# Listing's narrow one-hot tile with the position innermost becomes one with the position outermost, on one Trainium2 core

## The chip, the cores and the metric

One core of a Trainium2 chip runs the whole program. The metric is device time in microseconds (us) of one execution. PE is the matrix engine, PEld its weight loads, DVE, ACT and POOL the vector, scalar and GpSimd engines, SP the engine that issues most DMAs.

## The reference

```python
def reference(**kwargs):                      # x: 8 x 3072 x 256
    attn_out = real(fft(fft(x, axis=1), axis=2))
    x = attn_out.reshape(24576, 256)
    x = elu(x @ w_in) @ w_out                 # d_ff = 2048
    return _moe2_ref(x, w_gate, w1, w2)

def _moe2_ref(x, w_gate, w1, w2):             # 8 experts, d_ff = 1024
    cap = N // E                              # 3072 tokens per expert
    order = np.argsort(-(x @ w_gate).flatten())
    for idx in order:                         # greedy: best pair first, while the expert has room
        tok, e = int(idx) // E, int(idx) % E
        if assigned[tok] >= 0 or counts[e] >= cap:
            continue
        assigned[tok] = e
        counts[e] += 1
    for e in range(E):
        mask = assigned == e
        out[mask] = np.maximum(x[mask] @ w1[e], 0.0) @ w2[e]
    return out
```

## The kernel before

`moe1` (to about 1,990 us of the span) computes the Fourier transforms and the first layer pair and leaves the router's numbers in the tile `L` (token p + 128 j lies in partition p, column j, of 192 columns). `moe2` then does the experts one after another. For each of the eight rounds there are two streams of small work besides the matrix work:

- `select(i)` finds the round's expert and its threshold by bisection and gives every chosen token its rank in the expert's list. Line 393 and 394 split the rank into `ri` (rank modulo 128) and `qi` (rank divided by 128, below 24), which become `rb` and `qb`.
- `listing(i)` turns the ranks into a list: entry (r, q) of the result `idx` must be the number of the token with rank 128 q + r. It does so with one-hot tiles and matrix products, in 12 chunks `c` of 16 columns j. The wide tile `oh` (128 x 16 per partition, line 479) is 1 where r equals the token's `rb`. The narrow tile `oq` is 48 x 16 per partition: entries 24 to 47 are 1 where q equals the token's `qb` (line 473), entries 0 to 23 are that times the column number j (`jb`, line 474), and last entries 24 to 47 are multiplied in place by the partition number (`pcol`, line 475). `place` (line 452) then does 16 matrix products per chunk, one for each j, with `oh[:, :, j]` as weights (128 columns) and `oq[:, :, j]` as the operand that streams (48 columns), summed in PSUM.

In listing 0 nothing else runs on PE: POOL does line 474, the tiles are taken from the pool `ex` (names hh, hl, yh, yl), and one bank sums all 12 chunks. In listings 1 to 7 DVE does line 474, `oq` and `oh` have two buffers each in the pool `rt`, and the chunk's sum is added to `pj` at line 457. The product of chunk c is issued after the one-hots of chunk c + 1.

The order of the work around listings 1 to 7 is written out by a simple clock: `expert(i)` issues the products of an expert (line 553 into the hidden layer, 594 to 596 out of it) and, after each few, takes a step of `listing` or `select` if the clock's costs (`dve(750)`, `act(450)`, ...) say that their engines are free. These costs are constants in the code, so the order on each engine is fixed when the program is built. Line 531 transposes gathered tokens (`yg`), line 571 makes the low half `hl` of the hidden layer on DVE, line 434 and 440 split weights on POOL.

Of the kernel before, what the change touches and what calls it, by code (L numbers as in the profile page):

```python
# [11 lines left out]
BF16 = mybir.dt.bfloat16  # L12
I32 = mybir.dt.int32
U16 = mybir.dt.uint16
AF = mybir.ActivationFunctionType
OP = mybir.AluOpType
# [5 lines left out]
NJ = N // 128  # L22
# [139 lines left out]
def moe2(tc, yd, R, w1, w2, out):  # L162
    nc = tc.nc
# [4 lines left out]
    with ExitStack() as ctx:  # L168
        con = ctx.enter_context(tc.tile_pool(name="con2", bufs=1))
        ctx.enter_context(nc.allow_low_precision(reason="counts up to 2048 are exact in float16"))  # L170
        rt = ctx.enter_context(tc.tile_pool(name="rt", bufs=1))
        wp = ctx.enter_context(tc.tile_pool(name="wp", bufs=1))
        ex = ctx.enter_context(tc.tile_pool(name="ex", bufs=2))
# [4 lines left out]
        def rps(shape, dtype=F32):  # L178
            return psum.tile(shape, dtype, name="rps")

        pcol = con.tile([128, 1], F32, name="pcol")
        tri = con.tile([128, 128], BF16, name="tri")
        onesb = con.tile([128, NJ], BF16, name="onesb")
        io16 = con.tile([128, 128, 16], BF16, name="io16")
        jb = con.tile([128, NJ], BF16, name="jb")
# [38 lines left out]
        def small(name, w=1, dtype=F32, bufs=2):  # L224
            return rt.tile([128, w], dtype, name=name, bufs=bufs)
# [20 lines left out]
        def act(d):  # L246
            ck.act = max(ck.act, ck.pe + 200) + d

        def dve(d, after=0):
            ck.dve = max(ck.dve, ck.pe + 200, after) + d  # L250
# [3 lines left out]
        def after():  # L254
            return max(ck.dve, ck.act) + AF0

        def select(i):
# [99 lines left out]
            for g in range(2):  # L357
                for c in range(2):
                    nc.tensor.matmul(tt[:, 2 * g + c:2 * g + c + 1], ge[:, g, 96 * c:96 * c + 96], onesb[:, 0:1],
                                     start=True, stop=True)  # L360
# [19 lines left out]
            u1, u2 = rt.tile([128, NJ], F32, name="u1"), rt.tile([128, NJ], F32, name="u2")  # L380
# [7 lines left out]
            yield after()  # L388
            while i - 1 in st and not st[i - 1]["listed"]:
                yield None  # L390
            ri = rt.tile([128, NJ], I32, name="ri")
            qi = rt.tile([128, NJ], I32, name="qi")
            nc.vector.tensor_scalar(ri, ui, 127, None, op0=OP.bitwise_and)
            nc.vector.tensor_scalar(qi, ui, 7, None, op0=OP.arith_shift_right)
# [1 line left out]
            qb = rt.tile([128, NJ], BF16, name="qb")  # L396
# [16 lines left out]
        def listing(i):  # L413
            while i not in st:
                yield None
            rb, qb, wix = (st[i][n] for n in ("rb", "qb", "wix"))
            wr = [wp.tile([128, 2 * FE], F32, name="wr%d" % a) for a in range(2)]
            for a, src in enumerate((w1.rearrange("e (p c) f -> (e p) (c f)", c=2),
                                     w2.rearrange("e (p c) d -> (e p) (c d)", c=8))):
                nc.gpsimd.indirect_dma_start(out=wr[a], out_offset=None, in_=src,  # L420
                                             in_offset=bass.IndirectOffsetOnAxis(ap=wix[:, 0:1], axis=0))
            fetched = ck.pe
            pj = small("pj", 48)
            prev = None
            while now[0] < i - 1:
                yield None
            wsp = [wp.tile([128, 2 * FE], F32R, name=n, bufs=2) for n in ("w1h", "w1l", "w2h", "w2l")]

            def split():
                for c in range(2):  # L430
                    rv = wr[0].rearrange("p (c f k) -> p c k f", c=2, k=8)[:, c]
                    hv, lv = (t.rearrange("p (c k f) -> p c k f", c=2, k=8)[:, c] for t in wsp[0:2])
                    nc.scalar.activation(hv, rv, AF.Copy)
                    (nc.gpsimd if i else nc.vector).tensor_tensor(lv, rv, hv, op=OP.subtract)
                    act(950)
                    yield after()
                for c in range(2):
                    ws = slice(1024 * c, 1024 * c + 1024)
                    nc.scalar.activation(wsp[2][:, ws], wr[1][:, ws], AF.Copy)
                    nc.gpsimd.tensor_tensor(wsp[3][:, ws], wr[1][:, ws], wsp[2][:, ws], op=OP.subtract)  # L440
                    act(950)
                    yield after()

            parts = split()

            if i == 0:
                pl0 = psum.tile([128, 48], F32, name="acc20")

            def place(c, oh, oq):
                pl = rps([128, 48]) if i else pl0  # L450
                for j in range(16):
                    nc.tensor.matmul(pl, oh[:, :, j], oq[:, :, j], start=j == 0 and (i > 0 or c == 0),  # L452
                                     stop=j == 15 and (i > 0 or c == NC - 1))
                if i == 0:
                    return
                if c:
                    nc.vector.tensor_tensor(pj, pl, pj, op=OP.add)
                else:
                    nc.vector.tensor_copy(pj, pl)

            for c in range(NC):
                js = slice(16 * c, 16 * c + 16)
                if i:
                    oh = rt.tile([128, 128, 16], BF16, name="oh", bufs=2)
                    oq = rt.tile([128, 48, 16], BF16, name="oq", bufs=2)
                else:
                    oh = ex.tile([128, 128, 16], BF16, name=("yh", "yl")[c % 2])
                    oq = ex.tile([128, 48, 16], BF16, name="h%s%d" % ("hl"[c % 2], c // 2), bufs=1)

                def row(a, n):  # L470
                    return a[:, js].unsqueeze(1).to_broadcast([128, n, 16])

                nc.vector.tensor_tensor(oq[:, 24:48], io16[:, 0:24], row(qb, 24), op=OP.is_equal)
                (nc.vector if i > 0 else nc.gpsimd).tensor_tensor(oq[:, 0:24], oq[:, 24:48], row(jb, 24), op=OP.mult)
                nc.scalar.activation(oq[:, 24:48], oq[:, 24:48], AF.Copy, scale=pcol)
                dve(750)
                act(450)
                yield 0
                nc.vector.tensor_tensor(oh, io16, row(rb, 128), op=OP.is_equal)
                if prev:  # L480
                    place(*prev)
                prev = (c, oh, oq)
                dve(1300)
                if ck.pe > fetched + WAIT:
                    next(parts, None)
                yield after()
            place(*prev)
            while ck.pe < fetched + WAIT and i and not draining[0]:
                yield None
            if i:  # L490
                yield from parts
            st[i]["listed"] = True
            while now[0] < i - 1:
                yield None
            idx = small("idx", 24, I32)
            if i == 0:
                nc.vector.tensor_copy(pj, pl0)
            nc.vector.scalar_tensor_tensor(idx, pj[:, 0:24], 128.0, pj[:, 24:48], op0=OP.mult, op1=OP.add)
            plan[i] = dict(idx=idx, wr=wr)
            plan[i]["w"] = wsp  # L500
            if i:
                ahead()
            else:
                fetch(*queue.pop(0))
                out_y[0] += 1
            dve(100)
            yield after()
            yield from parts
# [4 lines left out]
        def ahead():  # L513
            while queue and out_y[0] < 3 and queue[0][0] in plan:
                fetch(*queue.pop(0))
                out_y[0] += 1

        def fetch(i, g):
            y = ex.tile([128, 4, YW], F32, name="yg", bufs=3)
            plan[i]["y", g] = y  # L520
            for t in range(4):
                nc.gpsimd.indirect_dma_start(
                    out=y[:, t], out_offset=None, in_=yd,
                    in_offset=bass.IndirectOffsetOnAxis(ap=plan[i]["idx"][:, 4 * g + t:4 * g + t + 1], axis=0))
# [90 lines left out]
        class Stream:  # L615
# [9 lines left out]
            def step(self):  # L625
# [6 lines left out]
                return False  # L632

        sel_s = Stream(select, E)
        lst_s = Stream(listing, E)

        def ready(i):
# [656 lines left out]
```

## Time and profile before

| | |
|---|---|
| time, median of 3 runs (lowest to highest) | 3475.95 us (3472.55 to 3478.8) |
| the profiled execution | 3493.99 us, its span 3492.2 us |
| busy share of the span: PE, PEld, DVE, ACT, POOL | 96%, 89%, 76%, 65%, 18% |
| chain that ended last, by engine | PE 85%, DVE 6%, ACT 4% |
| that chain's share on line 452 (into `rps`) | 3% |
| granted clock, mean over the span | 0.977 |

Busy time is the union of an engine's instructions; matrix products overlap in the pipeline, so a product's own duration is longer than its distance from the next one. "The distance" below is from the start of one product to the start of the next. [...] A row of the timeline merges equal neighbours: "x16" are 16 instructions, and the duration beside it runs from the start of the first to the end of the last.

### The profile page before, as it was taken

How to read it: one execution, taken by the hardware profiler on the slowest of the kernel's cores; microseconds unless marked ns; L12 is line 12 of the kernel's file. 1: busy time of each engine (PE TensorE's matmuls, PEld its weight loads, DVE VectorE, ACT ScalarE, POOL GpSimd, SP SyncE). 2: the span in 40 equal slices, each digit the busy share in tenths (PEclk: the TensorE clock that was granted, in tenths of full speed). 3: DMA queues.
4: the chain of work that ended last, by engine and by line, in shares of the span. 5: the costliest groups of instructions: out<-in, count | busy, mean ns of one | idle time of the engine just before them, and what ended most of it. 6: DMA issues, size and time to landing. Idle time of an engine off the chain costs nothing.

```text
span 3492.2 us, 62331 instructions
## 1 busy us (share of the span) xinstructions
PE 3343.3 (96%) x25472; PEld 3121.3 (89%) x25472; DVE 2637.7 (76%) x4930; ACT 2257.5 (65%) x3029; POOL 641.0 (18%) x837
## 2 busy tenths in 40 slices
PE   7999999999999999999999828999999999999999
PEld 4999999999999999999999827888798888888998
DVE  7888888888878888888878887677677777777522
ACT  4777777778777777777777736454546364645332
POOL 4000000000000000000000034333343334243432
PEclk9999999999999999999999958999999999999999
DMA  7112121121121111211100001111111111111110
GB/s 202 30 47 50 45 42 31 52 42 40 33 45 51 35 42 40 42 46 36 37 13 13 19 25 43 49 48 51 40 55 43 52 43 61 61 37 60 40 48 32
DMA packets 97075, 159.30 MB, mean 46 GB/s; under 512 B 18515, under 2 KB 68439, under 8 KB 94613
## 3 DMA queue, kind: packets, MB, share of 16 engines
q1 hardware_dynamic: 68357, 66.54, 7.8%
q0 software_dynamic: 24736, 80.42, 7.5%
q10 hardware_dynamic: 3696, 8.36, 0.7%
q8 instruction: 200, 3.28, 0.4%
q14 instruction: 86, 0.70, 0.1%
HBM read 91.78 MB, written 63.47 MB: 44 GB/s over the span
## 4 chain that ended last, share of the span: by engine, by line
PE 85%; DVE 6%; ACT 4%; issue 2%; DMA 1%; POOL 0%; another core or an unknown queue 0%; ACTq 0%; DVEq 0%; POOLq 0%; SPq 0%
PE hps L553 14%; PE acc L1116 11%; PE acc L1115 11%; PE acc L1114 11%; PE pq L1061 5%; PE pq L1063 5%; PE pq L1062 5%; PE acc L594 4%; PE acc L596 3%; PE acc L595 3%; PE rps L452 3%; ACT junk L289 3%; PE pq L1065 3%; PE pq L785 2%; PE pq L867 1%
## 5 line engine op out<-in xcount | busy, mean ns | idle before, releaser
L1116 PE MATMUL acc<-woh,gl 128*128 128x264 f32 x3072 | 876.1, 285 | 1.2 <-DVE gl L1101 1.1
L1115 PE MATMUL acc<-wol,gh 128*128 128x264 f32 x3072 | 875.2, 285 | 0.0
L1114 PE MATMUL acc<-woh,gh 128*128 128x264 f32 x3072 | 873.8, 284 | 1.3 <-DVE wol L1035 1.3
L1114 PEld LDWEIGHTS acc<-woh,gh 128*128 128x128 f32 x3072 | 578.9, 188 | 1.5 <-issue 1.5
L1116 PEld LDWEIGHTS acc<-woh,gl 128*128 128x128 f32 x3072 | 578.7, 188 | 1.7 <-DVE gl L1101 1.6
L1115 PEld LDWEIGHTS acc<-wol,gh 128*128 128x128 f32 x3072 | 577.8, 188 | 0.0
L1084 ACT ACTIVATE e<-h 128x1024 f32<-128x1024 f32 x384 | 408.5, 1064 | 158.5 <-DVE h L1078 158.1
L1077 DVE TENSOR_TENSOR h<-pq,qs 128x512 f32<-128x512 f32 x384 | 265.6, 692 | 287.9 <-ACT qs L1071 286.9
L1101 DVE TENSOR_TENSOR gl<-g,gh 128x1024 fp32r<-128x1024 f32 x384 | 468.4, 1220 | 1.6 <-ACT gh L1096 1.6
L1091 DVE SCALAR_TENSOR_TENSOR g<-e,h 128x1024 f32<-128x1024 f32 x384 | 467.5, 1218 | 0.1
L594 PE MATMUL acc<-w2h,hh 128*128 128x256 f32 x1536 | 455.9, 297 | 0.5 <-issue 0.4
L596 PE MATMUL acc<-w2h,hl 128*128 128x256 f32 x1536 | 435.0, 283 | 2.2 <-DVE hl L571 1.9
L595 PE MATMUL acc<-w2l,hh 128*128 128x256 f32 x1536 | 435.7, 284 | 0.0
L571 DVE SCALAR_TENSOR_TENSOR hl<-hps,hh 128x512 fp32r<-128x512 f32 x384 | 262.9, 688 | 216.6 <-ACT hh L565 195.8
L1086 ACT ACTIVATE e<-e 128x1024 f32<-128x1024 f32 x384 | 408.0, 1063 | 10.7
L1096 ACT ACTIVATE gh<-g 128x1024 fp32r<-128x1024 f32 x384 | 404.3, 1053 | 2.1 <-PE acc L1115 2.1
L1071 ACT ACTIVATE qs<-pq 128x512 f32<-128x512 f32 x384 | 230.2, 600 | 209.0 <-PE pq L1065 204.7
L565 ACT ACTIVATE hh<-hps 128x512 fp32r<-128x512 f32 x384 | 227.0, 594 | 200.1 <-PE hps L553 149.1
L604 POOL DMA_INDIRECT out<-osb,yg x192 | 203.6, 1060 | 621.6 <-ACT osb L601 591.5
L553 PE MATMUL hps<-yh,w1h 128*128 128x512 f32 x768 | 311.6, 406 | 2.0 <-DVE hl L571 1.9
L553 PE MATMUL hps<-yh,w1l 128*128 128x512 f32 x768 | 302.3, 394 | 0.0
L553 PE MATMUL hps<-yl,w1h 128*128 128x512 f32 x768 | 301.0, 392 | 0.0
(319 smaller groups left out, 7465.3 us busy)
## 6 DMA issues: line engine op xcount, KB each, us to landing
yd<-ysb SPq DMA_DIRECT2D x48, 514.0 KB
zd<-zev SPq DMA_DIRECT2D x29, 385.5 KB
xa<-x SPq DMA_DIRECT2D x28, 384.0 KB
zt<-zd SPq DMA_DIRECT2D x16, 193.5 KB
xa<-w_out ACTq DMA_DIRECT2D x6, 512.0 KB
zt<-zd SPq DMA_DIRECT2D x32, 96.0 KB
yg<-yd,idx POOLq DMA_INDIRECT x192
out<-osb,yg POOLq DMA_INDIRECT x192
```

The lines of the kernel that those rows point to most:

```text
L553: nc.tensor.matmul(ps, w[:, ws], v[:, c], start=c + k == 0, stop=c + k == 3)
L594: nc.tensor.matmul(acc[t // 2][:, t % 2], hh[:, ts], w2h[:, fs], start=f == 0, stop=False)
L595: nc.tensor.matmul(acc[t // 2][:, t % 2], hh[:, ts], w2l[:, fs], start=False, stop=False)
L596: nc.tensor.matmul(acc[t // 2][:, t % 2], hl[:, ts], w2h[:, fs], start=False, stop=f == 7)
L1084: nc.scalar.activation(e, st["h"], AF.Relu, scale=-1.0)
L1086: nc.scalar.activation(st["e"], st["e"], AF.Exp, scale=-1.0)
L1091: nc.vector.scalar_tensor_tensor(g, st["e"], -1.0, st["h"], op0=OP.add, op1=OP.max)
L1096: nc.scalar.activation(st["gh"], st["g"], AF.Copy)
L1101: nc.vector.tensor_tensor(st["gl"], st["g"], st["gh"], op=OP.subtract)
L1114: nc.tensor.matmul(o, st["gh"][:, i, ts], woh(c), start=c == 0, stop=False)
L1115: nc.tensor.matmul(o, st["gh"][:, i, ts], wol(c), start=False, stop=False)
L1116: nc.tensor.matmul(o, st["gl"][:, i, ts], woh(c), start=False, stop=c == 15)
```

## The change

The narrow tile is laid out as [16, 48] per partition, position j outermost, so that what streams for one j is 48 neighbouring elements. The comparison (now line 476) is made in a tile of its own in the old layout, `eqq`, [24, 16]; the product with `jb` (477) and the one with `pcol` (478) read `eqq` and write across into `oq` through a rearranged view `ov`. `eqq` has one buffer: in listings 1 to 7 a new tile of `rt`, in listing 0 the tile hl7 of `ex`. `ri` takes the buffer of `u1`, which makes the room in `rt`. The layout of `oh` is not touched.

```diff
-            ri = rt.tile([128, NJ], I32, name="ri")
+            ri = rt.tile([128, NJ], I32, name="u1")
...
-                    nc.tensor.matmul(pl, oh[:, :, j], oq[:, :, j], start=j == 0 and (i > 0 or c == 0),
+                    nc.tensor.matmul(pl, oh[:, :, j], oq[:, j], start=j == 0 and (i > 0 or c == 0),
...
-                    oq = rt.tile([128, 48, 16], BF16, name="oq", bufs=2)
+                    oq = rt.tile([128, 16, 48], BF16, name="oq", bufs=2)
...
-                    oq = ex.tile([128, 48, 16], BF16, name="h%s%d" % ("hl"[c % 2], c // 2), bufs=1)
+                    oq = ex.tile([128, 16, 48], BF16, name="h%s%d" % ("hl"[c % 2], c // 2), bufs=1)
...
-                nc.vector.tensor_tensor(oq[:, 24:48], io16[:, 0:24], row(qb, 24), op=OP.is_equal)
-                (nc.vector if i > 0 else nc.gpsimd).tensor_tensor(oq[:, 0:24], oq[:, 24:48], row(jb, 24), op=OP.mult)
-                nc.scalar.activation(oq[:, 24:48], oq[:, 24:48], AF.Copy, scale=pcol)
+                eqq = (rt.tile([128, 24, 16], BF16, name="eqq") if i else
+                       ex.tile([128, 24, 16], BF16, name="hl7", bufs=1))
+                ov = oq.rearrange("p j q -> p q j")
+                nc.vector.tensor_tensor(eqq, io16[:, 0:24], row(qb, 24), op=OP.is_equal)
+                (nc.vector if i > 0 else nc.gpsimd).tensor_tensor(ov[:, 0:24], eqq, row(jb, 24), op=OP.mult)
+                nc.scalar.activation(ov[:, 24:48], eqq, AF.Copy, scale=pcol)
```

No engine's instructions change their order or their count; shapes and waits do. In listing 0, DVE's rows before were these (compare of a chunk, then its wide one-hot; the names are the borrowed tiles):

```order
L473 TENSOR_TENSOR hh_24162<-io_23598,qb 128x384 [waits DMAHW1_49,DMAHW7_49,DMAHW0_49,DVE_49]
L479 TENSOR_TENSOR yh<-io_23598,rb 128x2048 [waits Activation_49]
L473 TENSOR_TENSOR hl_24168<-io_23598,qb 128x384
L479 TENSOR_TENSOR yl<-io_23598,rb 128x2048
L473 TENSOR_TENSOR hh_24190<-io_23598,qb 128x384
```

The same place with the change:

```order
L476 TENSOR_TENSOR hl_24163<-io_23598,qb 128x384 [waits DMAHW1_49,DMAHW7_49,DMAHW0_49,DVE_49]
L482 TENSOR_TENSOR yh<-io_23598,rb 128x2048 [waits Activation_49]
L476 TENSOR_TENSOR hl_24170<-io_23598,qb 128x384 [waits Activation_49,Pool_49]
L482 TENSOR_TENSOR yl<-io_23598,rb 128x2048
L476 TENSOR_TENSOR hl_24193<-io_23598,qb 128x384 [waits Activation_49,Pool_49]
```

From the second chunk on, the compare now waits for ACT and POOL, which read the one `eqq`. On ACT, in listing 0, line 475 stood so:

```order
L400 ACTIVATE rb<-ri 128x192 [waits DVE_49]
L475 ACTIVATE hh_24162<-hh_24162,pcol 128x384 [waits DMAHW3_49,DMAHW1_49,DMAHW7_49,DMAHW0_49,Pool_49]
L475 ACTIVATE hl_24168<-hl_24168,pcol 128x384 [waits Pool_49]
L475 ACTIVATE hh_24190<-hh_24190,pcol 128x384 [waits Pool_49]
L475 ACTIVATE hl_24213<-hl_24213,pcol 128x384 [waits Pool_49]
```

and with the change so:

```order
L400 ACTIVATE rb<-u_24143 128x192 [waits DVE_49]
L478 ACTIVATE hh_24162<-hl_24163,pcol 128x24x16 [waits DMAHW3_49,DMAHW1_49,DMAHW7_49,DMAHW0_49,DVE_49]
L478 ACTIVATE hl_24169<-hl_24170,pcol 128x24x16 [waits DVE_49]
L478 ACTIVATE hh_24192<-hl_24193,pcol 128x24x16 [waits DVE_49]
L478 ACTIVATE hl_24216<-hl_24217,pcol 128x24x16 [waits DVE_49]
```

ACT waited for POOL, whose input it overwrote; now it waits for DVE's compare alone.

## Rows read from the trace of the kernel before

**Rows 1.** Stretches: length, then PE, PEld, DVE, ACT, POOL busy us; clock; DMA.

```profile
2066.00:2100.00 34.00, 20.39 (x192) 19.00 (x192) 30.48 (x34) 10.39 (x15) 25.67 (x14) 0.50 0.15 55
2100.00:3282.00 1182.00, 1136.12 (x8103) 1000.08 (x8104) 849.55 (x2338) 613.10 (x1009) 443.90 (x520) 0.98 0.16 49
```

**Rows 2.** What PE waited for, 2100 to 3492 us: first of eleven rows of DMA and DVE.

```profile
PE tps L531 <- DMA yg<-yd,idx: 14.6, 10, 4.2
PE rps L298 <- DVE low L292: 9.3, 5, 3.5
```

**Rows 3.** Groups by line, 2100 to 3492 us: busy us, mean ns, idle before.

```profile
L452 PE MATMUL rps<-oq,oh 128*128 128x48 bf16 x1344 | 145.6, 279 | 1.7 <-DVE pj L457 1.7
```

**Rows 4.** Line 452 alone: count, duration min/median/max ns, first and last start.

```profile
L452 PEld LDWEIGHTS <-oh x1344: 142/148/180, 2216.4 to 3278.4; 128*128 128x128 bf16 x192
...
L452 PE MATMUL acc<-hh,yh x96: 255/279/288, 2070.7 to 2096.7; 128*128 128x48 bf16 x96
```

**Rows 5.** Lines 342 and 373, products with dense bf16 operands: durations as before.

```profile
L342 PEld LDWEIGHTS <-gm x96: 95/96/106, 2060.4 to 3206.4; 128*128 128x128 bf16 x96
L342 PE MATMUL rps<-wb,gm x96: 169/169/183, 2062.5 to 3206.4; 128*128 128x16 bf16 x96
...
L373 PE MATMUL rps<-ge,tri x8: 322/322/481, 2064.7 to 3210.0; 128*128 128x384 bf16 x8
```

**Rows 6.** Timeline of PE at 2062 us: start us, us, engine, line.

```profile
2062.55 0.47 PE L342 MATMUL rps<-wb,gm 128*128 128x16 bf16 x12 [1.97 <-DVE sgn L335]
```

**Rows 7.** Timeline of listing 0, its first three chunks.

```profile
2068.24 1.76 POOL L474 TENSOR_TENSOR hh<-hh,jb 128x384 bf16<-128x384 bf16 x1 [2.74 <-ACT rb L400]
2069.16 1.07 DVE L473 TENSOR_TENSOR hl<-io,qb 128x384 bf16<-128x384 bf16 x1
2069.29 0.14 PEld L452 LDWEIGHTS <-yh 128*128 128x128 bf16 x1 [3.89 <-DVE yh L479]
...
2070.30 1.83 POOL L474 TENSOR_TENSOR hl<-hl,jb 128x384 bf16<-128x384 bf16 x1 [0.29 <-DVE hl L473]
2070.71 1.70 PE L452 MATMUL acc<-hh,yh 128*128 128x48 bf16 x16 [4.94 <-ACT hh L475]
...
2072.43 1.84 POOL L474 TENSOR_TENSOR hh<-hh,jb 128x384 bf16<-128x384 bf16 x1 [0.29 <-DVE hh L473]
```

**Rows 8.** Timeline of a narrow window at the first group of listing 1.

```profile
2216.23 0.35 DVE L473 TENSOR_TENSOR oq<-io,qb 128x384 bf16<-128x384 bf16 x1
2216.36 0.21 PEld L452 LDWEIGHTS <-oh 128*128 128x128 bf16 x2 [0.23 <-DVE oh L479]
2216.37 0.29 PE L452 MATMUL rps<-oq,oh 128*128 128x48 bf16 x1
```

**Rows 9.** Groups of POOL by line, whole span.

```profile
L434 POOL TENSOR_TENSOR w1l<-wr,w1h 128x1024 fp32r<-128x1024 f32 x14 | 43.1, 3080 | 40.5 <-ACT w1h L433 40.4
L440 POOL TENSOR_TENSOR w2l<-wr,w2h 128x1024 fp32r<-128x1024 f32 x16 | 40.9, 2560 | 25.5 <-ACT w2h L439 25.4
...
L1132 POOL TENSOR_SCALAR L<-ysb 128x32 f32<-128x32 f32 x47 | 21.9, 467 | 1247.8 <-DVE ysb L1129 1201.0 <-DVE hm L159 38.6 <-DVE eo L771 8.2
```

**Rows 10.** Timeline of the end of listing 0.

```profile
2094.89 1.84 POOL L474 TENSOR_TENSOR hl<-hl,jb 128x384 bf16<-128x384 bf16 x1 [0.29 <-DVE hl L473]
...
2096.76 0.62 ACT L475 ACTIVATE hl<-hl,pcol 128x384 bf16<-128x384 bf16 x1 [1.52 <-POOL hl L474]
...
2097.43 1.72 PE L452 MATMUL acc<-hl,yl 128*128 128x48 bf16 x16 [0.43 <-ACT hl L475]
```

**Rows 11.** Timeline of the first chunk of listing 1.

```profile
2214.82 0.36 DVE L474 TENSOR_TENSOR oq<-oq,jb 128x384 bf16<-128x384 bf16 x1
2215.09 1.22 DVE L479 TENSOR_TENSOR oh<-io,rb 128x2048 bf16<-128x2048 bf16 x1
2215.21 0.62 ACT L475 ACTIVATE oq<-oq,pcol 128x384 bf16<-128x384 bf16 x1 [2.75 <-DVE oq L474]
```

**Rows 12.** Groups by line, 2100 to 3492 us: line 571 on DVE.

```profile
L571 DVE SCALAR_TENSOR_TENSOR hl<-hps,hh 128x512 fp32r<-128x512 f32 x384 | 262.9, 688 | 216.6 <-ACT hh L565 195.8 <-issue 17.2 <-ACT w2h L439 1.9
```

## The prediction

> **What bounds the kernel now.** I read the table of stretches first. Between 2100 and 3282 us, where listings 1 to 7 lie, PE is busy 1136.12 of 1182 us, DVE only 849.55 [rows 1]: the matrix engine sets the pace, and what it waits for is little. The waits of PE say how little: 14.6 us for gathered tokens, then seven rows with DVE as the cause, the largest 9.3 us, 18.3 us together [rows 2]. So there a nanosecond of PE is worth nearly a nanosecond, and one of DVE about 18.3 / 850, 2%. In listing 0, from 2066 to 2100 us, it is the other way round: PE is busy 20.39 us at the low clock, and the timeline shows a loop in which POOL's product hardly ever pauses (0.29 us between two of them) [rows 1, 7]. There the loop through POOL counts, not PE.
>
> Line 452 costs PE 145.6 us in 84 groups of 16, so 1.733 us each [rows 3]. Taking off the last product's 0.279 us and dividing by 15, a product follows the one before it after 97 ns. In listing 0, at clock 0.50, it is (1.70 - 0.279) / 15 = 95 ns [rows 1, 7]. The same at half the clock: the array's clock does not set it, the feeding does.
>
> **Which of the two operands sets the 97 ns.** Both `oh[:, :, j]` and `oq[:, :, j]` are read with a step of 32 bytes; only the second becomes dense.
> - What streams: dense products last 169 ns with 16 columns and 322 ns with 384, so 0.416 ns for a column and 182 ns for 48 [rows 5]. The shortest of line 452 in listing 0 lasted 255 ns [rows 4], and that is one for which no weights were waited for: in the first group they had been loaded at 2069.29 us and the product ran at 2070.71 us [rows 7]. So reading 48 columns across costs 255 - 182 = 73 ns more than reading them dense, and with the dense 20 ns it takes about 93 ns, which is the whole distance.
> - The weights: a strided load lasts 148 ns, a dense one 96 ns [rows 4, 5]: 52 ns more. Twelve products with dense weights stand (0.47 - 0.169) / 11 = 27 ns apart [rows 5, 6], so the strided load occupies its path for at most 27 + 52 = 79 ns. From below: at the start of a group the load begins at 2216.36 us, and the first product (from 2216.37 us) lasts 0.29 us, some 35 ns more than the 255 ns without a wait [rows 4, 8]; so the weights served after about 45 ns.
>
> So today the streamed operand sets the distance and the weights hide behind it. Afterwards the weights set it.
>
> [...]
>
> **The change part by part, and the sum.**
> 1. *Products in listings 1 to 7.* The new distance lies between 45 and 79 ns, or stays at 97 ns if I have the wrong operand. I take 72 ns: the 52 ns are the measured extra of such a load, and of the 27 ns, which hold the issue too, I give the load 20. That saves 25 ns in 84 x 16 = 1344 products: -33.6 us. Ends: 52 ns saved, -70 us; none, 0.
> 2. *Listing 0, POOL's product writes across.* One chunk takes 2072.43 - 2070.30 = 2.13 us now [rows 7]. Each compare there lasts 1.07 us beside POOL's product where one alone lasts 0.35 us [rows 7, 8], so in fact it already ends with that product. With one `eqq` it must start after it: POOL's product t, a hop of 0.03 us (2096.73 to 2096.76 [rows 10]), 0.35 us, a hop of 0.07 us (2070.23 to 2070.30 [rows 7]): t + 0.45 us. For t: 1.84 us if the writing costs nothing. The nearest row for one operand with a wide step is line 434, which reads every eighth number of `wr`, against line 440, dense: 3080 - 2560 = 520 ns in 1024 elements, 0.5 ns each, 0.2 us in 384 [rows 9]. I take t = 2.04 us, so 2.49 us a chunk: 11 x 0.36 + 0.2 = +4.2 us. From above, line 1132, which picks runs of 8 numbers, needs 467 ns for 32, 14.6 ns each with its fixed part [rows 9]: t = 5.6 us, 11 x 3.9 + 3.8 = +47 us; far off in shape, and kept as an end.
> 3. *The end of listing 0.* `pcol`'s product no longer waits for POOL; today it stands between POOL's end at 2096.73 us and PE's start at 2097.43 us [rows 10]. It goes beside POOL: -0.6 us. The last group of PE there gets 16 x 23 ns shorter: -0.4 us. The other eleven groups lie beside POOL.
> 4. *DVE's product with `jb` in listings 1 to 7.* 384 elements take 0.36 us, 2048 take 1.22 us [rows 11]: 0.52 ns each, 0.16 us fixed. Line 571 (f32) takes 688 ns for 512, so 1.03 ns each over the same fixed part [rows 12]. Written across I expect the slower rate: 0.56 us, +0.2 us x 84 = 16.8 us of DVE. With 2% of DVE on the path, +0.4 us. Ends: 0 and, if every chunk held PE, +16.8 us.
> 5. *ACT's product with `pcol`, written across.* 0.62 us now [rows 11]. ACT is busy 613 of 1182 us [rows 1], so half a microsecond more would be hidden. Nothing.
> 6. *The wait for the one `eqq` in listings 1 to 7.* Behind a waiting compare stand the wide one-hot and the `hl` of line 571, for which PE waits. But in the tightest of the 77 places ACT's product ends at 2215.83 us [rows 11] and the next compare begins at 2216.23 us [rows 8]: 0.4 us to spare, and the slower product of DVE adds 0.2 to it. Nothing; without that cover up to 0.6 us a chunk. `ri` in `u1`'s buffer: both are written by DVE, in order: nothing.
>
> Sum: -33.6 + 4.2 - 1.0 + 0.4 = -30.0 us. The profiled execution took 3493.99 us, so it would take 3464; it lies 18.0 us above the median of the runs. From the median, 3475.95 - 30.0 = **3446 us**, 0.9% less.
>
> **The rivals.**
> - *The weights already set the 97 ns* (the two reads hinder each other, or the 255 ns hold something else). Then PE gains nothing and the costs stand: +3.6 us, 3480 us; from t = 2.3 us on it is slower by over 0.2% (7 us, about what runs of this kernel can tell from no change), and at t = 5.6 us it is 3522 us. For it: in the median its products last 279 ns [rows 3], 24 ns more than the 255 ns, so something besides the stream is waited for. Against it: the 255 ns themselves, without any load to wait for. This is the rival on the other side; it decides if the distance falls by less than 3 ns. Chance 0.15, half of it over the 0.2%.
> - *The weights serve early*, at 45 ns, as at the start of a group: -70 + 3.6, 3410 us. Against it: no load lasted under 142 ns [rows 4], so the next one probably finds its path taken. Chance 0.13.
> - *Strided weights cost nothing once the stream is dense*: the distance falls to the 27 ns of line 342, 70 x 1344 = 94 us, 3385 us. Against it stand the 148 ns of the load. Chance 0.04. [...]
> - *The gain is handed back*: PE, 34 us earlier, meets gathers (14.6 us of waits already [rows 2]) and `hl` sooner; half is lost, 3462 us. Against it: in 2100 to 3282 us DVE has 332 us free [rows 1]. Chance 0.13.
>
> **How the numbers follow.** The forecast has 0.55. Its own range is 3434 (distance 62 ns) to 3460 us (79 ns and t = 2.5 us). The range of 8 in 10 is 3405 to 3474 us: it takes in the early weights and the half lost, and leaves out the 27 ns and the case without gain. Faster by over 0.2%: 0.55 + 0.13 + 0.04 + 0.13 = 0.85, less 0.02 for costs at their upper ends, 0.83; within 0.2%: 0.09; slower: 0.08.
>
> **What would show it.** In the new profile line 452 in listings 1 to 7 should stand 72 ns apart (group about 1.3 us instead of 1.73), its products shorter than 279 ns, while the loads keep 148 ns. POOL's product in listing 0 should last near 2.0 us and a chunk 2.5 us; the compare there 0.35 us after a wait for POOL. DVE's product should last 0.56 us and PE's waits for DVE should stay near 18 us. The prediction is wrong if the distance stays above 90 ns, if POOL's product lasts over 4.8 us (then listing 0 loses what PE gains), or if the waits for `yg` grow by tens of us.

## The result, and the profile after

The change makes the kernel slower: 3523.75 us (3519.1 to 3524.41) against 3476.59 us (3472.55 to 3478.8) on the same chip, a ratio of 1.0134, 95% interval 1.0117 to 1.0152: +47 us where the prediction had -30. A later set of runs gave 1.0145 (1.0129 to 1.0160).

Groups by line from the first gather to the end (the counterpart of [rows 3]), first the two products as they were before:

```profile
L475 ACT ACTIVATE oq<-oq,pcol 128x384 bf16<-128x384 bf16 x84 | 51.9, 618 | 139.2 <-DVE oq L474 130.2 <-DVE oq L473 8.4
L474 DVE TENSOR_TENSOR oq<-oq,jb 128x384 bf16<-128x384 bf16 x84 | 35.6, 424 | 2.9
```

With the change, these two, line 452 and the compare:

```profile
L477 DVE TENSOR_TENSOR oq<-eqq,jb 128x384 bf16<-128x384 bf16 x84 | 184.1, 2191 | 2.9
L478 ACT ACTIVATE oq<-eqq,pcol 128x384 bf16<-128x384 bf16 x84 | 181.3, 2159 | 137.4 <-DVE eqq L476 137.1
...
L452 PE MATMUL rps<-oq,oh 128*128 128x48 bf16 x1344 | 99.1, 222 | 11.5 <-DVE pj L457 11.4
...
L476 DVE TENSOR_TENSOR eqq<-io,qb 128x384 bf16<-128x384 bf16 x84 | 51.0, 608 | 0.2
```

PE got what was promised, and more: the 1344 products take 99.1 us, not 145.6, so they stand (99.1 / 84 - 0.222) / 15 = 64 ns apart instead of 97. But the two products that write across take a mean of 2.19 us on DVE (0.42 before) and 2.16 us on ACT (0.62). The compare of line 476 waited for 0.2 us in all 84 chunks, so the single `eqq` holds nobody up in listings 1 to 7.

Listing 0, its first two chunks on the timeline (the counterpart of [rows 7]):

```profile
2063.07 0.36 DVE L476 TENSOR_TENSOR hl<-io,qb 128x384 bf16<-128x384 bf16 x1
...
2063.47 2.10 ACT L478 ACTIVATE hh<-hl,pcol 128x384 bf16<-128x384 bf16 x1 [0.49 <-DVE hl L476]
2063.58 2.86 POOL L477 TENSOR_TENSOR hh<-hl,jb 128x384 bf16<-128x384 bf16 x1 [2.74 <-ACT rb L400]
...
2066.47 0.36 DVE L476 TENSOR_TENSOR hl<-io,qb 128x384 bf16<-128x384 bf16 x1 [1.90 <-POOL hh L477]
...
2066.91 2.92 POOL L477 TENSOR_TENSOR hl<-hl,jb 128x384 bf16<-128x384 bf16 x1 [0.47 <-DVE hl L476]
...
2069.86 0.36 DVE L476 TENSOR_TENSOR hl<-io,qb 128x384 bf16<-128x384 bf16 x1 [1.90 <-POOL hl L477]
```

A chunk is POOL's 2.92 us and 0.47 us of waiting, 3.39 us where it was 2.13. From the first compare to the first gather it is 45.5 us (2063.07 to 2108.61) instead of 32.1.

Stretches (columns as in [rows 1]). Before, from the first gather to the end, and 64 us that hold listing 2:

```profile
2099.90:3492.20 1392.30, 1340.26 (x9445) 1187.36 (x9445) 908.08 (x2416) 674.21 (x1105) 508.97 (x620) 0.99 0.15 48
...
2388.00:2452.00 64.00, 63.46 (x482) 57.77 (x480) 45.67 (x76) 26.16 (x38) 21.32 (x19) 1.00 0.09 32
```

With the change: listings 1 to 7; the whole from the first gather to the end; 71 us that hold listing 2; two short ones that are spoken of below; and the whole again in e5, a second profile of the change:

```profile
2108.60:3303.00 1194.40, 1109.90 (x8089) 963.21 (x8089) 978.72 (x2335) 726.00 (x1007) 460.01 (x518) 0.97 0.15 48
2108.60:3516.90 1408.30, 1317.75 (x9445) 1153.51 (x9445) 1038.68 (x2417) 788.06 (x1105) 526.32 (x620) 0.98 0.15 47
2392.00:2463.00 71.00, 59.53 (x481) 51.69 (x480) 65.57 (x77) 41.63 (x39) 23.95 (x19) 1.00 0.08 28
...
2740.00:2754.50 14.50, 11.90 (x87) 10.20 (x87) 13.57 (x16) 9.96 (x8) 6.10 (x6) 1.00 0.08 29
2754.50:2761.30 6.80, 6.39 (x29) 4.42 (x28) 6.01 (x10) 5.33 (x7) 4.14 (x3) 0.50 0.14 39
...
2112.60:3539.10 1426.50, 1322.96 (x9445) 1157.35 (x9445) 1040.57 (x2416) 787.61 (x1105) 524.05 (x620) 0.97 0.15 47
```

In the 71 us DVE is busy for 65.57 and PE for 59.53; the same work took 64 us before, with 45.67 of DVE and 63.46 of PE. DVE has taken PE's place as the engine that sets the pace there. Over the whole stretch, 1392.3 us with 1340.26 us of PE before, the account of the first profile is: line 452 has 46.5 us less busy, the other work of PE 24.0 us more (1317.75 - 99.1 against 1340.26 - 145.6; a few us of it are group ends that overlapped their neighbours), and PE stands idle for 90.5 us instead of 52.0. That is +16 us; listing 0 adds 13.4, and it starts 4.7 us earlier (2063.07 instead of 2067.74 us). So the two spans differ by 24.7 us, not by 47. These two profiles are no good pair: that of before took 3493.99 us, 17 us above the median, but as long as the kernel before takes on the chips of e1 to e8 (3491.4 and 3492.7 us). The profile of e5, the change on such a chip, has a span of 3539.2 us and shows the whole 47.0 us: listing 0 takes 45.5 instead of 32.1 us (+13.4), line 452 is 46.4 us less busy (99.2), the other work of PE is 29.1 us more, and PE stands idle for 103.5 us instead of 52.0 (+51.5).

What PE waited for, first gather to end (the counterpart of [rows 2]):

```profile
PE hps L556 <- DVE hl L574: 22.5, 15, 6.1
PE tps L534 <- DMA yg<-yd,idx: 14.5, 10, 4.2
PE rps L271 <- DVE pj L457: 13.1, 5, 4.2
PE rps L452 <- DVE pj L457: 11.4, 7, 3.5
PE acc L599 <- DVE hl L574: 4.8, 6, 2.6
```

These four rows of DVE come to 51.8 us, all eight of DVE's to 56.7; before, all of them were 18.3 us, of which 9.3 at line 298 are missing in this profile. In e5, which has these too (9.0), DVE's rows come to 69.3 us: 51.0 more than before, nearly all of the 51.5 us of added idle time. The wait for gathers is what it was (14.6). One such place, on the timelines of DVE, ACT and PE:

```profile
2750.12 1.97 DVE L477 TENSOR_TENSOR oq<-eqq,jb 128x384 bf16<-128x384 bf16 x1
2752.75 0.69 DVE L574 SCALAR_TENSOR_TENSOR hl<-hps,hh 128x512 fp32r<-128x512 f32 x1 [0.66 <-ACT hh L568]
...
2750.18 2.11 ACT L478 ACTIVATE oq<-eqq,pcol 128x384 bf16<-128x384 bf16 x1 [2.49 <-DVE eqq L476]
2751.77 0.95 ACT L568 ACTIVATE hh<-hps 128x512 fp32r<-128x512 f32 x1
...
2753.50 0.50 PE L556 MATMUL hps<-yh,w1h 128*128 128x512 f32 x1 [2.60 <-DVE hl L574]
...
2754.98 0.63 PE L556 MATMUL hps<-yl,w1h 128*128 128x512 f32 x1
```

The slow writes of DVE and ACT stand in their queues ahead of `hh` (568) and `hl` (574); in the two short stretches above PE is busy 11.90 of 14.50 us, and then the granted clock, 1.00 before, stands at 0.50, half of full speed, for 6.8 us, where a product of line 556 takes 0.63 instead of 0.39 us. So here a wait is followed by slower products. Counted in steps of 2 us, the granted clock stands at 0.50 for some 41 us of the stretch before, 70 us after, 88 us in e5, and 70 us in e8, which adds nothing but work of DVE. At 0.50 the products of line 556 start 0.43 us apart (2754.55 and 2754.98 us) where at 1.00 it is 0.23 us (2762.20 and 2762.43 us), nearly twice as far; so by estimate 29 and 47 us more of it could be up to 15 and 24 us of the 24.0 and 29.1 us by which PE's other work grew. Whether a wait for DVE brought any of these stretches on is not shown.

### The profile page after: what moved, and what is told of

The parts are those of the page before. It is cut to its first block, busy times and chain, and to the rows that moved or that the text cites. A ratio compares the mean times of both kernels' runs of the same rounds, so it can differ in the third digit from the quotient of the medians.

```text
span 3516.9 us, 62349 instructions
## 1 busy us (share of the span) xinstructions
PE 3311.7 (94%) x25472; PEld 3080.3 (88%) x25472; DVE 2762.8 (79%) x4930; ACT 2388.1 (68%) x3029; POOL 671.6 (19%) x837
## 4 chain that ended last, share of the span: by engine, by line
PE 77%; DVE 12%; ACT 6%; issue 2%; POOL 1%; DMA 1%; ACTq 0%; SPq 0%; DVEq 0%; POOLq 0%
PE hps L556 12%; PE acc L1119 11%; PE acc L1118 11%; PE acc L1117 11%; PE pq L1064 5%; PE pq L1066 5%; PE pq L1065 5%; ACT junk L289 3%; PE pq L1068 3%; PE acc L597 3%; PE acc L599 2%; PE acc L598 2%; DVE oq L477 2%; PE pq L788 2%; DVE oh L482 1%
## 5 line engine op out<-in xcount | busy, mean ns | idle before, releaser
L607 POOL DMA_INDIRECT out<-osb,yg x192 | 214.5, 1117 | 611.5 <-ACT osb L604 588.0
```

## The experiments

The theory (A): a write across is slow by itself on each engine, and DVE's and ACT's lateness reaches PE. Rivals: (B) DVE and ACT, writing halves of one tile at once, hinder each other; (C) the single `eqq`; (D) PE's gain isn't worth its face. Ratios are to the kernel before on the chip of that set; the sets were e1 to e4, e5 to e8 and e9 to e12, with 3491.4, 3492.7 and 3477.6 us for before.

**e1: the instructions by themselves.** 384 bf16 elements written with steps of 2 to 128 bytes, f32 across, bf16 read across; then series of products.

> This kernel leaves out the whole computation; it repeats single instructions, five times each, one engine after the other, and then 12 series of 16 products for each of four layouts. Theory A (writing 2-byte numbers across is slow by itself, on each engine): with 384 elements and a step of 96 bytes, DVE's product alone lasts 1.9 to 2.1 us against 0.36 dense, ACT's 2.0 to 2.2 us against 0.62, POOL's 2.8 to 3.0 us against 1.8; with DVE and ACT at once in two halves of one tile it is no longer than alone. Theory B (it is slow because DVE and ACT write interleaved halves of one tile at the same time): alone both last under 0.8 us, and only the part with both at once shows 2 us. Within A, the series of steps from 2 to 128 bytes tells what it hangs on: if on leaving dense order at all, a step of 4 bytes is as slow as one of 96; if on landing in a new line of memory, the time climbs up to some step and then stays; a 4-byte element at 96 bytes is as slow as a 2-byte one if the line counts, and near 0.56 us if the half word counts. Reading across and writing dense should stay under 0.7 us on DVE if only the writing side is slow. PE: strided weights with a strided operand 97 ns apart, strided weights with a dense operand 62 to 64 ns, dense weights with a strided operand about 93 ns if the operand's reading sets it, both dense about 27 ns.

DVE (min/median/max ns); `d_step` has, in this order, steps of 2, 4, 8, 16 and 32 bytes, the two `d_wrap` rows 48 and 96, `d_wrapf` is f32 at 96:

```profile
L63 DVE TENSOR_TENSOR d_step<-eqq,jb x4: 294/357/359, 5.5 to 6.7; 128x384 bf16<-128x384 bf16 x4
L63 DVE TENSOR_TENSOR d_step<-eqq,jb x5: 578/585/586, 7.3 to 9.8; 128x384 bf16<-128x384 bf16 x5
L63 DVE TENSOR_TENSOR d_step<-eqq,jb x4: 999/1010/1011, 10.3 to 13.4; 128x384 bf16<-128x384 bf16 x4
L63 DVE TENSOR_TENSOR d_step<-eqq,jb x4: 1855/1856/1900, 15.3 to 21.0; 128x384 bf16<-128x384 bf16 x4
L63 DVE TENSOR_TENSOR d_step<-eqq,jb x4: 1759/1760/1982, 24.3 to 29.9; 128x384 bf16<-128x384 bf16 x4
L63 DVE TENSOR_TENSOR d_wrap<-eqq,jb x3: 1919/1919/1919, 35.3 to 39.2; 128x384 bf16<-128x384 bf16 x3
L63 DVE TENSOR_TENSOR d_wrap<-eqq,jb x3: 1970/1970/1971, 54.0 to 58.0; 128x384 bf16<-128x384 bf16 x3
L63 DVE TENSOR_TENSOR d_wrapf<-eqq,jb x5: 1105/1106/1325, 70.9 to 75.7; 128x384 f32<-128x384 bf16 x5
L63 DVE TENSOR_TENSOR d_readacross<-d_src,jb x5: 1099/1103/1106, 77.6 to 82.2; 128x384 bf16<-128x384 bf16 x5
...
L86 DVE TENSOR_TENSOR both<-eqq,jb x5: 1970/1971/1972, 252.1 to 260.1; 128x384 bf16<-128x384 bf16 x5
```

From a step of 4 bytes over 8 to 16 the median goes from 585 over 1010 to 1856 ns, and from 32 to 96 bytes it is 1760 to 1970 ns: for these 2-byte numbers the time goes with the number of 16-byte pieces that the write touches. With the 0.16 us fixed part of the prediction, steps of 4, 8 and 16 bytes touch 96, 192 and 384 pieces and give (0.585 - 0.16) / 96, (1.01 - 0.16) / 192 and (1.856 - 0.16) / 384, 4.4 ns each time. Reading across, or writing 4-byte numbers across, both at a step of 96 bytes, costs about half of that, (1.10 - 0.16) / 384 = 2.4 ns a number. With ACT writing the other half of the same tile at the same time DVE needs 1971 ns, alone 1970: rival B falls. ACT goes from 614 to 2105 ns, POOL from 908 to 2006 ns alone, and to 2317 to 2967 ns beside DVE's wide one-hot (2.92 us in listing 0). Three expectations missed: reading across was to stay under 0.7 us on DVE (1.10), f32 across was to take either what 2-byte numbers take or 0.56 us (1.11), and POOL alone 2.8 to 3.0 us (2.0).

PE, weights and operand across (ss), operand dense (sd), weights dense (ds), both dense (dd); first and last start:

```profile
L118 PE MATMUL p_ss<-mst,wst x192: 260/278/288, 302.9 to 321.2; 128*128 128x48 bf16 x192
L118 PE MATMUL p_sd<-mde,wst x192: 221/235/239, 321.3 to 333.1; 128*128 128x48 bf16 x192
L118 PE MATMUL p_ds<-mst,wde x192: 246/268/268, 333.2 to 350.1; 128*128 128x48 bf16 x192
L118 PE MATMUL p_dd<-mde,wde x192: 182/183/221, 350.2 to 356.2; 128*128 128x48 bf16 x192
```

Over 191 distances: 96, 62, 88 and 31 ns. The operand across sets the distance by itself (88 ns with dense weights), then the weights do (62 ns). The granted clock was 0.68, 0.50, 0.50 and 0.72 in these four series; the kernel has nearly the first two distances at 1.00 (97 and 64 ns), while the 31 ns are not a figure for 1.00.

**e2: all dense in the new layout.** The comparison is made in the new layout too, so nothing writes across.

```diff
-                nc.vector.tensor_tensor(eqq, io16[:, 0:24], row(qb, 24), op=OP.is_equal)
-                ....tensor_tensor(ov[:, 0:24], eqq, row(jb, 24), op=OP.mult)
-                nc.scalar.activation(ov[:, 24:48], eqq, AF.Copy, scale=pcol)
+                nc.vector.tensor_tensor(eqq, q24, col(qb), op=OP.is_equal)
+                ....tensor_tensor(oq[:, :, 0:24], eqq, col(jb), op=OP.mult)
+                nc.scalar.activation(oq[:, :, 24:48], eqq, AF.Copy, scale=pcol)
```

> The narrow tile keeps the new layout, but the comparison is made in that layout too, so that all three instructions write dense. Theory A (the writes across are the whole cost): products stay 64 ns apart, DVE's product goes back to about 0.36 us and ACT's to about 0.62 us, PE keeps its 46 us of gain, and listing 0 costs 0 to 4 us for the wait of the one comparison tile: 3476 - 46 + 2 = about 3432 us, 3425 to 3450. Theory B (DVE and ACT collide in one tile): both still write halves of one tile at once, so their products stay near 2 us and the time near 3520 us. Theory C (the wait for the single comparison tile is what costs): that wait stands here too, so the time stays near 3520 us. Rival D (PE's gain is not worth its face, since PE then waits for gathers or the hidden layer): 3455 to 3470 us.

Ratio 0.9938 (0.9924 to 0.9951), -21.4 us. The products stand 64 ns apart as in the change, ACT's lasts 0.615 us, so B falls, and with the 0.2 us of waiting above C too; but it is half of the gain that A expected. The compare and DVE's product last 0.55 and 0.56 us at best, not 0.35 and 0.36 (one source is now a number that is read 24 times in a row; no run shows whether that is the cause), 0.4 us more a chunk. Whether that or rival D took the rest is for e8 to e11.

**e3: across, but the products as before.** `oq` keeps the layout of before; the comparison is made with the position outermost, so both products write across with 32 bytes.

> The price of writing across without PE's gain: the narrow tile has the layout of before, so the products read it with a step of 32 bytes as before, and the comparison is made with the position outermost, so that both products write across with a step of 32 bytes. Theory A: products stay 97 ns apart; if a step of 32 bytes is as slow as one of 96, DVE's and ACT's products last about 2 us and POOL's 2.9 us, and the time is that of the change plus PE's lost gain, 3524 + 46 = 3570 us, less what PE's slower pace covers of DVE's lateness, so 3530 to 3570 us. If the cost hangs on the step and 32 bytes are cheap, 3478 to 3495 us. Theory C (only the wait for the single comparison tile): about 3520 us with short products.

Ratio 1.0206 (1.0192 to 1.0220), +72 us, DVE's product 2.12, ACT's 2.04 us, products 97 ns apart. This is the price of the writes without PE's gain; with it (the change, 1.0145 in e5, where DVE is about as busy from the first gather on: 1040.57 us, here 1045.88) it is 0.0061 or 21 us less, where 33 ns x 1344 = 44 us are saved on PE.

**e4: listing 0 as before, listings 1 to 7 as in the change; e5: the change again.**

> Listing 0 as before, listings 1 to 7 as in the change. From the traces listing 0 grew from 32.1 to 45.5 us, so all theories in which that stretch is on the path give 3524 - 13.4 = 3510 us (3506 to 3515), still 1.0% slower than before: the rest, 47 - 13 = 34 us, is lost in listings 1 to 7. If listing 0's loss is given back later (the first gathers would only wait for something else), 3524 us; if listing 0 were the whole loss, below 3480 us.

> The change itself once more, so that the partial kernels beside it have it on their own chip. All theories: about 1.0134 of before (1.0117 to 1.0152), and one more profile of it; the 24.7 us by which the first two profiles' spans differ is expected to split again into about -41 us on line 452 (what its products take from the path after the first gather), +13 us in listing 0 and the rest in idle time of the matrix engine and in slower products of the other lines at the lower clock.

e4 1.0104 (1.0088 to 1.0119), e5 1.0145. Listing 0 is worth 0.0030 against the first measurement and 0.0041 against e5: 10 to 14 us, as its 13.4 us on the timeline. The loss in listings 1 to 7 is larger.

**e6 and e7: one of the two across.** In e6 only the product with `jb`, in e7 only that with `pcol`; the other is dense in place, for which DVE makes one more comparison.

> Only the product with the column number (on DVE, in listing 0 on POOL) writes across; ACT's is dense in place, for which DVE makes one more comparison (0.56 us) in the new layout. Theory A1 (DVE's lateness is what costs, ACT's is hidden): DVE has per chunk 0.35 + 0.56 + 2.0 us, 0.5 us more than in the change, so the time is that of the change or above it: 1.013 to 1.025 of before, ACT's product 0.62 us. Theory A2 (ACT's late product is what costs): with ACT dense the time falls to 1.000 of before or under it.

> Only ACT's product writes across (2.1 us); the product with the column number is dense in place, for which a second comparison in the new layout is made (0.56 us). DVE has per chunk 0.35 + 0.56 + 0.56 us against 0.35 + 2.0 in the change, POOL in listing 0 again 1.83 us. Theory A1 (ACT's lateness is hidden): near the kernel in which all is dense (0.994 of before), plus the 0.35 us comparison: 0.994 to 1.001. Theory A2 (ACT's late product costs): 1.008 to 1.013.

e6 1.0178 (1.0164 to 1.0192), e7 1.0040 (1.0026 to 1.0053). With DVE across and ACT dense it is no faster than the change, but its further comparison makes DVE 35.3 us busier than in e5 (1075.82 - 1040.57), 14 us at e8's price, and it takes 11.5 us more. So beside DVE's lateness ACT's seems hidden, but for some 3 us at that price; the extra comparison keeps e6 from showing it outright. And e7 lies above my 0.994 to 1.001: against e2 it costs 36 us more. Of these, 2 us are in listing 0 (36.1 against 34.1), and 25.8 us more of DVE (968.60 - 942.85 in the stretches from the gather) are 10 us at e8's price. So most of the rest, some 24 us, is ACT's product, which does reach PE when DVE isn't late. PE's waits for `hl`, first e2, then e7:

```profile
PE hps L559 <- DVE hl L577: 6.6, 7, 3.5
```

```profile
PE hps L561 <- DVE hl L579: 19.4, 13, 4.9
```

The two delays don't simply add: the change with both is 72 us above e2, and e6 without ACT's is still 84 above it.

**e8 and e11: DVE's time priced alone.** The kernel before, with five further comparisons a chunk in listings 1 to 7, and with one.

```diff
+                if i:
+                    eqq = rt.tile([128, 24, 16], BF16, name="eqq")
+                    for _ in range(5):
+                        nc.vector.tensor_tensor(eqq, io16[:, 0:24], row(qb, 24), op=OP.is_equal)
```

> The kernel before, with five further comparisons per chunk of listings 1 to 7 into a tile that nobody reads: 5 x 0.35 = 1.75 us of DVE a chunk, 84 x 1.75 = 147 us in all, and nothing else changed (the products stay as they were, listing 0 too). This prices DVE's time where the prediction priced it at 2%. By the prediction's 2%: +3 us, 1.001. By its upper end (every chunk holds the matrix engine): +147 us, 1.042. By what the all-across kernel with the old products cost (1.0206, of which some 10 us in listing 0, for about 170 us of DVE): about a third, +50 us, 1.014.

> The kernel before with one further comparison per chunk of listings 1 to 7 (0.35 us, 84 x 0.35 = 29 us of DVE): a small dose beside the one of five, about the extra 0.4 us a chunk that the dense form in the new layout costs. If the price of DVE's time is the same from the first microsecond on (0.40): +12 us, 1.0034. If small delays are absorbed and only large ones reach the matrix engine (the prediction's 2%): under 1.0005.

e8 1.0169 (1.0155 to 1.0183), by the ratio +59 us (54 by the medians) for about 147 us of DVE, 0.40 us each; e11 1.0015 (1.0006 to 1.0024), +5 us for 29.5, 0.18 each, between what its two theories gave (1.0034 and under 1.0005). By the intervals that is 0.07 to 0.28 against 0.37 to 0.43: the price rises with the dose, and already the first is several times 2%. What PE waits for in e8 are the same lines as in the change, without any write across:

```profile
PE hps L557 <- DVE hl L575: 19.5, 13, 6.0
PE tps L535 <- DMA yg<-yd,idx: 14.5, 10, 4.2
PE rps L271 <- DVE pj L457: 8.8, 3, 5.1
```

**e9: e2 with listing 0 as before; e10: the same with the `jb` product on POOL in listings 1 to 7.**

> Listings 1 to 7 in the new layout, all three instructions dense; listing 0 as before. Against the kernel with all of it dense (0.9938 of before) this gives back what its listing 0 lost: 34.1 us from the first compare to the first gather against 32.1 us before, so -2 us: 0.993 (0.992 to 0.9945). If listing 0 is not on the path: 0.994.

> As the kernel with listing 0 as before and dense listings 1 to 7, but there the product with the column number is on POOL (0.91 us alone, 1.83 us in listing 0) instead of DVE. DVE then has per chunk one comparison of 0.55 us, less than the 0.71 us of before. If DVE's time is what ate PE's gain, at 0.38 us of path for each us of DVE (five comparisons: 147 us cost 0.0169 of 3492, 59 us, so 0.40), 0.56 x 77 = 43 us less of DVE give 17 us: 0.988 of before (0.985 to 0.991), and PE's waits for the hidden layer's low half fall below 4 us. Rival: POOL is behind its weight splits (2.5 to 3.1 us each) and slows DVE's instructions beside it (the comparison lasted 1.07 us beside POOL's product in listing 0): 0.993 to 1.002.

e9 0.9927 (0.9913 to 0.9940), 3452.86 us, 24.7 us faster than before: the fastest version here. e11 and e9 stand on one chip, have the same listing 0 and about the same extra DVE work (0.35 and 0.4 us a chunk) and differ mainly by PE's gain: 3482.35 - 3452.86 = 29.5 us of 44. (ACT's product also waits for one instruction of DVE less in e9; that part is not separated.) e10 failed, outside both its ranges: 1.0052 (1.0038 to 1.0065), since POOL does it late.

```profile
PE rps L452 <- POOL oq L480: 37.8, 10, 10.0
PE tps L541 <- DMA yg<-yd,idx: 14.0, 10, 3.8
PE hps L563 <- DVE hl L581: 9.6, 7, 3.6
```

So e10 doesn't tell what the gain would be with less of DVE.

**e12: read across, written dense.**

> The comparison stays in the old layout, dense; the two products read it across (a step of 32 bytes) and write dense. From the single instructions: 1.10 us on DVE and 1.24 us on ACT reading across, against 1.97 and 2.11 writing across. DVE has per chunk 0.35 + 1.10 us against 0.55 + 0.56 in the all-dense kernel, 0.34 us more: 29 us of DVE, at 0.40 us 11 us, and listing 0's chunk is POOL's 1.15 to 1.9 us + 0.45: 0.994 + 0.003 = 0.997 (0.995 to 1.001). If only the change of layout and no rate counted: 1.0145.

0.9956 (0.9943 to 0.9970): with the same transposition done on the reading side the change is a gain.

```profile
L481 ACT ACTIVATE oq<-eqq,pcol 128x384 bf16<-128x384 bf16 x84 | 88.1, 1049 | 120.7 <-DVE eqq L479 120.4
L480 DVE TENSOR_TENSOR oq<-eqq,jb 128x384 bf16<-128x384 bf16 x84 | 83.4, 993 | 2.9
```

## Why the prediction was wrong

The account from single edits: new layout, dense (e9) -0.0073; the writes across in listings 1 to 7 (e9 to e4) +0.0177; listing 0 (e4 to the change) +0.0030 to +0.0041. The sum, +0.0134 to +0.0145, is the change by construction, since each step starts where the one before ends; what the steps show is the size of each. The middle one also swaps e9's comparison of 0.55 us for one of 0.35, so it understates the price of the writes.

1. *Products: right, and undersized.* The streamed operand sets the 97 ns, the weights come next (e1: 88 ns with only the operand across, 62 ns with only the weights); 64 ns instead of 72, within 45 to 79 (62 ns would have given 3433 us as the low end, not 3434). One reading was off without harm: the 255 ns are from listing 0 at clock 0.50, the dense 182 ns from 1.00. The dense product of 384 columns lasts 481 ns at 0.50 instead of 322, 0.41 ns more for a column, so 48 dense columns would last 202 ns there: reading across costs 53 ns more, not 73, but on top of 40 ns, which again makes 93. But of 44 us on PE 29.5 reach the end (e9 against e11), 21 when DVE is late (e3): "a nanosecond of PE is worth nearly a nanosecond" failed too, and the rival "handed back" was partly true.
2. *Listing 0: the form right, t wrong.* A chunk is t + 0.47 us (predicted t + 0.45), but t is 2.92, not 2.04 us: +13.4 instead of +4.2 us. The row that I took, line 434, reads f32 numbers with a step; here 2-byte numbers are written with one. Having DVE beside it is not the reason: from dense to across POOL's product grows by 1.08 us in listing 0 (1.84 to 2.92) and by 1.10 us alone (908 to 2006 ns in e1).
3. *The end of listing 0: the mechanism held.* ACT starts beside POOL there, and PE starts 0.05 us after POOL's end (2106.69 to 2106.74) instead of 0.70. ACT's product grew to 2.1 us, but ends before POOL's.
4. *DVE's product: the step that failed most*, in both factors. "Written across I expect the slower rate: 0.56 us" took line 571's dense f32 for a price of scattered writes; it is 1.97 us at least, by 4.7 ns an element. DVE is busy for 978.72 us, not 849.55, in listings 1 to 7: some 129 us more, not 16.8. And "with 2% of DVE on the path" divided present waits by present work. That average says what DVE costs while it is early; the price of more is 0.18 for the first 29 us and 0.40 over 147 us (e11, e8). By the measured factors the term is about 129 x 0.40 = 52 us, not 0.4. The 0.40 is from a kernel with PE's slow products; from e9 to e4, with the quick ones, 100 us more of DVE (941.29 to 1041.45) cost 62 us, ACT's late product included.
5. *ACT's product: wrong.* 2.16, not 0.62 us; and "half a microsecond more would be hidden" holds, but for a few us, only behind DVE's lateness (e6), not without it (e7).
6. *The single `eqq`: right.* 0.2 us of waiting in 84 chunks, and e2 keeps it and gains.

What stays open: what makes 2-byte numbers written across nearly twice as dear as 4-byte ones (e1: 1.97 against 1.11 us for 384 on DVE, at a step of 96 bytes), how much of the loss is the clock's, whether ACT's late product costs anything beside DVE's, and what PE's gain is worth with DVE no later than before.

## What to carry to other kernels

Here the transposition cost something on whichever side it was done: price it with an instruction of that step and element size, written or read, before trading. In e1, at 96 bytes, reading across cost 2.4 ns an element on DVE, and writing 2-byte elements across, at the steps listed there from 16 to 96 bytes, 4.2 to 4.7. And the price of an engine that isn't the bottleneck is read from the stretch in which it gets the work (in listing 2 DVE had 64 - 45.67 = 18 us free for 12 chunks, 1.5 us each, and the change asked for 1.6), not from the average of its waits; a spare instruction repeated in the kernel before measures it.

## What the runs showed that I had not expected

- DVE's time for 2-byte numbers written across goes by the 16-byte pieces that they touch, 4.4 ns a piece at steps of 4, 8 and 16 bytes, where a 4-byte number at a step of 96 bytes costs 2.4 ns (e1).
- POOL and DVE slow each other in e1: POOL's write across takes 2.0 us alone and up to 2.97 us beside DVE's wide one-hot, and that one up to 2.36 instead of 1.22 us (e1).
- The kernel before took 3476.6, 3491.4, 3492.7 and 3477.6 us in the four sets of runs, 0.5% apart, so only ratios within a set are compared.
